# Attention weights spread by transfers from SBUF to SBUF instead of matmuls and copies, in three chunks of four

## The chip, the cores and the metric

One Trainium2 chip, one core. The time is device time in microseconds (us) of one execution, as a median over runs. PE is the matrix engine (TensorE), PEld its weight loads, DVE the vector engine, ACT the scalar engine, POOL the GpSimd engine, SP the engine that only issues transfers. Each engine works through its own queue strictly in order and waits on semaphores for the others. Matmuls write to PSUM, of which there are eight banks of 128 x 512 float32.

## The reference

A transformer layer on 2048 positions of width 512, in bfloat16: attention over a sliding window, then a gated MLP, each after a layer norm and with a residual.

```python
qkv = (x @ wqkv)...                         # 32 heads of 16
off = jnp.arange(8) * 2                     # W = 8 places back, step 2
logits = einsum("bhsd,bhswd->bhsw", q, kg) * scale     # kg: k at pos - off
attn = softmax(where(mask, logits, -1e9))
o = einsum("bhsw,bhswd->bhsd", attn, vg)    # then @ wo
...
h = x + A(layernorm(x));  gate = relu(layernorm(h) @ W_gate)
h2 = h + (gate * (layernorm(h) @ W_up)) @ W_down       # F = 1376
```

Each position sees only itself and seven earlier positions, two apart. So scores and weighted sums are element-wise products of shifted rows, not matmuls of queries by keys.

## The kernel before

The 2048 positions are cut into four chunks of 512 (`tk` 0 to 3). Within a chunk, activations stand transposed: features on partitions, positions along the row. The features are put in an order such that one tile (t = 0 to 3) of 128 partitions holds 4 of each head's 16 dimensions, partition 4h + q belonging to head h.

Per chunk the steps are, with their names in the code (`key`, written here as step and chunk, mu3.2 for `mu`, tile 3, chunk 2):

- Layer norm of x: `xst`, `xag` (DVE statistics), `xrl`, `xre` (ACT, reciprocal root as exp of a log), `xxn` (DVE, normalised rows), then the transpose: `xtp` on PE with `xte` on ACT, or `xtd` as a transposing DMA issued by SP (L472). The list DMAT names which pairs of blocks go by DMA: x of chunk 3, h of chunks 2 and 3, and half of h of chunk 1 (`htd`).
- Projections `qkv0` to `qkv11` (L524; q and k first, then v) with their copies `qe` on ACT (L532).
- Scores: `pr0`, `pr1` (two each, DVE, L571) multiply q by four shifted views of k, 128 x 4096 at a time, into a `big` buffer; `sc0`, `sc1` (PE, L577) sum over dimensions with 0/1 weights, in column tiles of 32; `ex0`, `ex1` take the exponential, giving two tiles `ex`, in which partition 32w + h holds the weight of window place w and head h.
- Normalisation: `den` (PE, L610) sums over the places, `dl` and `dr` (ACT) make the reciprocal; in chunks 1 to 3 (EARLY) `am0`, `am1` (DVE, L625) multiply the weights by it.
- Spread: the weights of a place stand on 32 partitions, one per head, and are wanted on 128, each four times. `bc0`, `bc1` (PE, L638) do it with four matmuls each, on row tiles of 32, into four PSUM banks; `be` (ACT, L644, four for each) copies the banks into a `big` buffer `ab` of 128 x 8 x 512.
- Weighted sum: `mu0` to `mu3` (DVE, L659) multiply `ab` by eight shifted views of v into a `big` buffer each; a tree of adds follows (`tree`, 4 + 2 + 1 wide; L662, L685). In chunks 0 to 2 (DACC) the first, widest add is an accumulating DMA issued by POOL (`ta`, L691, 512 KB).
- `wo` (PE, L711) and the residual `rs`, layer norm of h (`hnm`, `hsq`, `hrl`, `hre`, `hxn`, `htp` or `htd`), then the MLP: `mm` (PE, L749, up and gate, 22 steps of four matmuls), `ue`, `ge` (ACT), `gu` (DVE), `dn` (PE, L786, two parts for each of four row blocks), `o` (DVE, L797, adds the residual) and `os` (a store, L801).

The order is not that of the loops. Every step is added to a plan with its engine, duration, latency, buffers taken and used; the list RANK gives each step a place, in the order in which steps are added. Each engine's queue is its steps sorted by RANK. `Plan.order` then walks the queues with the planned durations, only to choose which buffer of a pool a step gets and in which order the program is written. So planned costs do not change an engine's order as long as RANK is there. Pools that matter here: five `big` buffers (products of scores, `ab`, and products with v share them), eight PSUM banks.

The last chunk's last row block is stored in two halves (`parts`), so the stores there are `os0` to `os4`.

Of the kernel before, what the change touches and what calls it, by code (L numbers as in the profile page):

```python
# [8 lines left out]
P = 128  # L9
BF16 = mybir.dt.bfloat16  # L10
# [3 lines left out]
ALU = mybir.AluOpType  # L14
# [4 lines left out]
    0, 1, 2, 3, 4, 5, 6, 7, 8, 9, 10, 11, 12, 13, 14, 15, 16, 18, 19, 24,  # L19
    26, 31, 32, 17, 20, 22, 23, 25, 29, 34, 35, 28, 33, 37, 39, 41, 45, 48, 21, 27,  # L20
    30, 36, 38, 42, 44, 46, 63, 74, 40, 56, 68, 49, 51, 54, 43, 60, 72, 53, 66, 65,
    77, 70, 83, 75, 80, 90, 92, 87, 114, 102, 110, 85, 105, 93, 104, 115, 125, 129, 78, 88,
    95, 99, 103, 183, 193, 202, 132, 143, 150, 156, 152, 106, 109, 116, 123, 119, 168, 181, 216, 220,
    224, 180, 188, 217, 223, 231, 187, 196, 226, 229, 234, 162, 172, 201, 205, 207, 237, 240, 239, 245,
    247, 251, 242, 248, 243, 246, 252, 256, 259, 263, 250, 254, 265, 266, 272, 278, 269, 276, 285, 275,
    283, 273, 280, 286, 318, 322, 292, 301, 304, 314, 313, 324, 341, 311, 325, 298, 303, 334, 338, 326,
    330, 346, 354, 360, 337, 355, 317, 353, 347, 358, 370, 329, 352, 340, 348, 332, 345, 294, 350, 356,
    361, 374, 343, 365, 372, 381, 351, 362, 413, 357, 368, 367, 386, 418, 400, 425, 460, 464, 417, 427,
    457, 467, 376, 434, 446, 466, 410, 429, 437, 668, 55, 61, 52, 57, 50, 58, 47, 59, 62, 64,
    67, 84, 73, 82, 86, 71, 81, 69, 79, 89, 166, 175, 122, 136, 111, 130, 137, 190, 91, 101,  # L30
    127, 173, 149, 179, 94, 96, 163, 213, 158, 170, 98, 107, 108, 167, 208, 197, 249, 257, 244, 235,
    255, 260, 264, 268, 274, 296, 279, 302, 309, 305, 310, 307, 287, 295, 290, 293, 300, 319, 328, 364,
    369, 315, 320, 359, 363, 335, 342, 380, 382, 327, 336, 373, 375, 389, 395, 387, 392, 396, 402, 393,
    399, 398, 401, 397, 403, 405, 409, 404, 407, 411, 412, 416, 419, 420, 423, 421, 428, 422, 426, 431,
    474, 482, 441, 443, 458, 463, 453, 468, 483, 438, 448, 436, 452, 442, 451, 450, 454, 456, 488, 492,
    479, 498, 455, 487, 491, 500, 507, 461, 493, 445, 459, 481, 485, 471, 475, 496, 511, 539, 524, 533,
    520, 535, 526, 530, 541, 514, 540, 484, 502, 543, 544, 556, 581, 589, 538, 552, 559, 562, 549, 554,
    584, 587, 529, 547, 560, 564, 113, 120, 100, 124, 76, 117, 97, 112, 128, 133, 140, 144, 142, 146,
    164, 145, 154, 148, 157, 161, 209, 230, 174, 186, 198, 200, 195, 215, 182, 184, 199, 228, 189, 211,
    169, 177, 178, 194, 232, 241, 271, 281, 185, 191, 261, 253, 284, 297, 289, 282, 308, 312, 321, 331,  # L40
    339, 344, 378, 366, 377, 371, 379, 383, 385, 394, 388, 391, 390, 430, 439, 470, 490, 424, 432, 473,
    476, 440, 447, 486, 489, 406, 415, 465, 477, 501, 518, 497, 504, 508, 512, 494, 499, 521, 525, 517,
    519, 516, 522, 503, 505, 527, 528, 532, 546, 534, 537, 536, 548, 531, 542, 579, 597, 566, 594, 585,
    601, 561, 580, 609, 599, 603, 588, 592, 571, 575, 577, 600, 605, 606, 610, 595, 623, 602, 611, 582,
    614, 627, 558, 576, 574, 578, 568, 572, 565, 567, 583, 621, 648, 639, 645, 636, 649, 591, 616, 652,
    624, 635, 628, 633, 640, 655, 663, 665, 667, 632, 654, 661, 711, 650, 656, 707, 710, 644, 657, 659,
    669, 126, 138, 118, 134, 131, 139, 121, 135, 141, 147, 155, 160, 151, 171, 159, 165, 153, 176, 203,
    236, 218, 225, 192, 204, 214, 219, 258, 291, 262, 270, 222, 233, 267, 277, 227, 238, 212, 221, 288,
    316, 206, 210, 306, 299, 323, 333, 384, 349, 408, 414, 433, 435, 444, 462, 449, 506, 510, 509, 513,
    515, 469, 495, 478, 472, 480, 563, 570, 586, 593, 523, 551, 557, 569, 573, 590, 596, 598, 545, 550,  # L50
    553, 555, 615, 622, 604, 607, 612, 619, 608, 613, 626, 629, 618, 620, 630, 631, 617, 625, 634, 637,
    638, 641, 646, 653, 643, 651, 642, 647, 691, 695, 681, 692, 694, 698, 688, 697, 700, 679, 687, 674,
    677, 670, 680, 666, 671, 690, 673, 675, 672, 682, 658, 662, 660, 678, 683, 684, 689, 664, 685, 699,
    702, 676, 693, 705, 701, 706, 704, 709, 686, 703, 708, 713, 715, 716, 718, 696, 714, 719, 720, 722,
    724, 731, 712, 726, 732, 734, 717, 725, 727, 730, 728, 733, 735, 737, 721, 723, 729, 736,
# [3 lines left out]
class Op:  # L59


    __slots__ = ("eng", "dur", "lat", "fn", "deps", "prio", "take", "use", "start", "done", "seq", "key")

    def __init__(self, eng, dur, fn, deps=(), prio=0.0, take=(), use=(), lat=0.0):
        self.eng, self.dur, self.fn, self.lat = eng, dur, fn, lat
        self.deps = [d for d in deps if d is not None]
        self.prio, self.take, self.use = prio, list(take), list(use)
        self.start = self.done = None
# [23 lines left out]
class Plan:  # L92
# [23 lines left out]
    def order(self):  # L116
# [14 lines left out]
        while left:  # L131
# [36 lines left out]
            op.start, op.done = t, t + op.dur + op.lat  # L168
            free[op.eng] = t + op.dur
# [18 lines left out]
def kernel(  # L188
# [20 lines left out]
    PADL = 16  # L209
    SCALE = DH ** -0.5  # L210
# [45 lines left out]
    big_s = slots(5, [P, W, CS], BF16, "big")  # L256
    gT_s = slots(7, [P, 2, CS], BF16, "gT")
    ex_s = slots(3, [P, CS], BF16, "ex")
    ln_s = slots(1, [P, CS], F32, "lnd")
# [81 lines left out]

    RPE, OPE = (0,), ()
# [5 lines left out]
    HG = ([[0, 1, 2, 3]],) * 4  # L348

# [3 lines left out]
    MM, TP = 0.2165, 0.07  # L353
    SW = 0.22
    PEL = 0.22
    A5, A10, AX, AS = 0.52, 0.92, 0.8, 0.24
    AL = 0.14
    D2, D5, D10, D20, D40, DST, DSM = 0.34, 0.62, 0.62, 1.15, 2.2, 0.63, 0.08
    DXN = 0.38
    DL = 0.14  # L360

    def load(t):
        return add(None, "LD", 0.0, None, lat=t)

    xload = [[load(t) for t in (3.4, 3.4, 4.2, 4.2)]] + [[load(t)] * BPC for t in (9.5, 14.0, 15.5)]
    wload = {n: load(t) for n, t in
             (("q", 8.0), ("k", 8.0), ("v", 12.0), ("o", 17.5), ("u", 21.5), ("g", 25.5), ("d", 29.5))}
# [17 lines left out]
    def layernorm(tk, src, dst_slots, pr, groups, on_act, residual=None):  # L385
# [7 lines left out]
        for grp in groups:  # L393
# [3 lines left out]
            for j in grp:  # L397
                if residual:
# [14 lines left out]
                    ag.append(add((ln + "sq" + gk, tk), "ACT", A5 + 0.1 if h else 0.73, f_sq, [a], pr,  # L413
# [52 lines left out]
            for j0 in range(lo, hi, step):  # L466
                if (ln, tk, j0) in DMAT:
                    for j in range(j0, min(j0 + step, hi)):
                        xn, a = norm(j)

                        def f_td(j=j, xn=xn):
                            nc.sync.dma_start_transpose(out=dst.t[:, :, j * P:(j + 1) * P], in_=xn.t[:])  # L472

                        evs.append(add((ln + "td" + gk, tk), "SP", TDD, f_td, [a], pr, take=[dst], use=[xn], lat=TDL))
                    continue
# [25 lines left out]
                evs.append(add((ln + ("tv" if tev else "te") + gk, tk), "DVE" if tev else "ACT", A10 if n == 2 else A5, f_ev, ds, pr, take=[dst], use=[tp], lat=AL))  # L501
# [5 lines left out]
    for tk in range(NCK):  # L507
# [49 lines left out]
        for hf in range(2):  # L557
# [26 lines left out]
            if tk in MERGE:  # L584
# [23 lines left out]
        def f_dn(exs=exs, dn=dn, tk=tk):  # L608
            for hf in range(2):
                nc.tensor.matmul(dn.t[:], lhsT=(same if tk in EARLY else spread)[:], rhs=exs[hf].t[:], start=(hf == 0), stop=(hf == 1))  # L610
# [7 lines left out]
        b = add(("den", tk), "PE", 2 * MM, f_dn, exd, apr + 2, take=[dn], use=exs, lat=PEL)  # L618
# [11 lines left out]
        ab, abd = Buf(big_s), []  # L630
        for w0 in range(0, W, BCN):
            hf = w0 // 4
            bcs = [Buf(at_s) for _ in range(BCN)]
# [17 lines left out]
        for t in range(NT):  # L651
# [35 lines left out]
            for n, du in ((4, D20), (2, D10), (1, D2)):  # L687
                f = lambda n=n, mt=mt, f=f_a: f(n, mt)
                if n == 4 and (tk, t) in DACC:
# [3 lines left out]
                    m = add(("ta%d" % t, tk), "POOL", 1.5, f_da, [m], tpr, use=[mt], lat=DAL)  # L693
# [3 lines left out]
                else:  # L697
                    m = add(("tree%d" % t, tk), "DVE", du, f, [m], tpr, use=[mt], lat=0.03)
# [7 lines left out]
        for j in range(BPC):  # L706
# [20 lines left out]
            if tk in RPE:  # L727
                a = add(("rs%d" % j, tk), "ACT", A5 + 0.1, f_rs, [a], base + 50, take=[sm], use=[od], lat=AL)
            else:
                a = add(("rs%d" % j, tk), "DVE", D5 + 0.1, f_rs, [a], base + 50, take=[sm], use=[od], lat=DL)  # L730
# [7 lines left out]
        for f0 in range(0, NFT, 2):  # L738
# [3 lines left out]
            for ft in fts:  # L742
# [4 lines left out]
                def f_mm(w_sb, mm, ft=ft, fs=fs, hnT=hnT):  # L747
                    for dt in range(NT):
                        nc.tensor.matmul(mm.t[:fs, :], lhsT=w_sb[:, dt, ft * P: ft * P + fs],  # L749
                                         rhs=hnT.t[:, dt, :], start=(dt == 0), stop=(dt == NT - 1))  # L750
# [4 lines left out]
                def f_ge(gm=gm, gr=gr, fs=fs, i=ft - f0):  # L755
                    nc.scalar.activation(out=gr.t[:fs, i, :], in_=gm.t[:fs, :], func=ACT.Relu)  # L756

                a = add(("mm%d" % (f0 // 2), tk), "PE", 4 * MM, lambda f=f_mm, um=um: f(wu_sb, um), hev + [wload["u"]], pr,
                        take=[um], use=[hnT], lat=PEL)
# [94 lines left out]
```

## Time and profile before

| | |
|---|---|
| time, median of 3 runs | 203.77 us (203.76 to 203.87) |
| span of the profiled execution | 200.7 us, 3.1 us less than the median time |
| granted PE clock | 0.999 |
| last matmul ends | 197.17 us |
| L638 spread matmuls | x32 (8 steps of 4) |
| L644 copies of the spread banks, ACT | x32, 17.8 us busy |
| L691 accumulating transfers, POOL | x12, 512 KB, 5.6 us from issue to landing |
| L801 stores, SP | x17, issue 0.33 to 0.48 us, 1.6 to 1.9 us to landing |
| L472 transposes, SP | x14, issue 1.20 to 2.14 us, 2.4 to 5.6 us to landing |

The page gives the span, from the first to the last instruction of the profiled execution, but no separate time for it; the difference of 3.1 us to the median of the runs lies around the span. In the lines below, a group is: line, engine, operation, output tile <- input tiles, shape, count; in the timeline the first two numbers are the start and the time in us, and the bracket tells how long the engine had idled and for whom. In the slices each digit is the busy tenth of one fortieth of the span, about 5 us. In the waits: engine, line, whom it waited for, total us, times, longest.

### The profile page before, as it was taken

How to read it: one execution, taken by the hardware profiler on the slowest of the kernel's cores; microseconds unless marked ns; L12 is line 12 of the kernel's file. 1: busy time of each engine (PE TensorE's matmuls, PEld its weight loads, DVE VectorE, ACT ScalarE, POOL GpSimd, SP SyncE). 2: the span in 40 equal slices, each digit the busy share in tenths (PEclk: the TensorE clock that was granted, in tenths of full speed). 3: DMA queues.
4: the chain of work that ended last, by engine and by line, in shares of the span. 5: the costliest groups of instructions: out<-in, count | busy, mean ns of one | idle time of the engine just before them, and what ended most of it. 6: DMA issues, size and time to landing. Idle time of an engine off the chain costs nothing.

```text
span 200.7 us, 2938 instructions
## 1 busy us (share of the span) xinstructions
PE 193.4 (96%) x1095; PEld 96.2 (48%) x1115; DVE 153.3 (76%) x239; ACT 121.8 (61%) x256; POOL 12.7 (6%) x28
## 2 busy tenths in 40 slices
PE   8999999989999999999999999999999999999992
PEld 8776445445445344444444444444444444444451
DVE  6989998989999999999996868799967412022313
ACT  3576798747899965887436779701566631277400
POOL 4000000410000013100131000000000000000000
PEclk9999999999999999999999999999999999999999
DMA  6989933994000009920399400131010050200103
GB/s 204 322 245 409 388 119 66 170 201 87 3 0 0 3 0 183 195 40 3 57 178 193 124 3 0 29 75 52 3 52 0 0 104 3 78 0 0 52 0 105
DMA packets 17676, 18.81 MB, mean 94 GB/s; under 512 B 8352, under 2 KB 14464, under 8 KB 17664
## 3 DMA queue, kind: packets, MB, share of 16 engines
q1 hardware_dynamic: 15360, 11.57, 18.5%
q0 software_dynamic: 1728, 6.29, 16.6%
q10 hardware_dynamic: 576, 0.79, 1.2%
q8 instruction: 8, 0.13, 0.3%
q14 instruction: 4, 0.03, 0.0%
HBM read 8.42 MB, written 2.10 MB: 52 GB/s over the span
## 4 chain that ended last, share of the span: by engine, by line
PE 67%; DVE 16%; DMA 6%; ACT 5%; issue 2%; SPq 1%; ACTq 0%
PE bank L749 29%; PE bank L524 15%; PE bank L786 14%; DVE big L659 6%; PE bank L711 5%; DMA quad<-row 5%; DVE big L571 3%; DVE gT L769 2%; DMA x_sm<-in_A_x_dram 1%; SPq L472 1%; PE bank L483 1%; DVE x_sm L722 1%; DVE big L662 1%; DVE row L454 1%; PE bank L577 1%
## 5 line engine op out<-in xcount | busy, mean ns | idle before, releaser
L749 PE MATMUL bank<-quad,wu_sb 128*128 128x512 bf16 (+1 forms) x172 | 42.4, 379 | 0.4
L749 PE MATMUL bank<-quad,wg_sb 128*128 128x512 bf16 (+1 forms) x173 | 42.0, 379 | 0.4 <-DMA quad<-row 0.3
L756 ACT ACTIVATE gr<-bank 128x512 bf16<-128x512 f32 (+1 forms) x44 | 25.3, 616 | 24.7 <-PE bank L749 22.9
L786 PE MATMUL bank<-wd_sb,gT 128*128 128x512 bf16 (+2 forms) x183 | 39.8, 366 | 0.2
L753 ACT CAST up_sb<-bank 128x512 bf16<-128x512 f32 (+1 forms) x44 | 25.0, 600 | 21.0 <-PE bank L749 17.3
L571 DVE TENSOR_TENSOR big<-quad,kT 128x4096 bf16<-128x4096 bf16 x16 | 36.2, 2284 | 0.2
L659 DVE TENSOR_TENSOR big<-big,vT 128x4096 bf16<-128x4096 bf16 x16 | 35.9, 2281 | 0.0
L769 DVE TENSOR_TENSOR gT<-gr,up_sb 128x1024 bf16<-128x1024 bf16 (+1 forms) x24 | 15.3, 642 | 24.0 <-ACT up_sb L753 14.4
L524 PE MATMUL bank<-quad,wqk_sb 128*128 128x512 bf16 (+1 forms) x139 | 29.9, 355 | 1.0 <-DMA quad<-row 0.8
L786 PEld LDWEIGHTS <-gT 128*128 128x128 bf16 (+1 forms) x187 | 18.1, 98 | 19.7 <-issue 0.4
L749 PEld LDWEIGHTS <-wg_sb 128*128 128x128 bf16 (+1 forms) x176 | 17.3, 100 | 21.2 <-issue 0.9
L749 PEld LDWEIGHTS <-wu_sb 128*128 128x128 bf16 (+1 forms) x176 | 17.5, 100 | 20.6 <-issue 0.7
L524 PEld LDWEIGHTS <-wqk_sb 128*128 128x128 bf16 x144 | 15.6, 114 | 12.8 <-issue 2.3
L797 DVE TENSOR_TENSOR row<-x_sm,bank 128x512 bf16<-128x512 bf16 (+1 forms) x17 | 10.6, 649 | 10.4 <-PE bank L786 10.4
L644 ACT CAST big<-bank 128x512 bf16<-128x512 f32 x32 | 17.8, 635 | 0.4 <-PE bank L638 0.2
L662 DVE TENSOR_TENSOR big<-big 128x1024 bf16<-128x1024 bf16 (+2 forms) x24 | 16.8, 728 | 0.1
L691 POOL DMA_DIRECT2D big<-big x12 | 10.5, 873 | 88.1 <-DVE big L659 59.9
L524 PE MATMUL bank<-quad,wv_sb 128*128 128x512 bf16 x62 | 15.6, 380 | 0.2
L711 PE MATMUL bank<-wo_sb,quad 128*128 128x512 bf16 x62 | 15.2, 379 | 0.2
L454 DVE TENSOR_SCALAR row<-x_sm,mv,rs 128x512 bf16<-128x512 bf16 x32 | 11.4, 407 | 3.7 <-ACT rs L436 3.1
L532 ACT CAST quad<-bank 128x512 bf16<-128x512 f32 x16 | 9.5, 612 | 4.6 <-PE bank L524 4.6
L499 ACT COPY quad<-bank 128x1024 bf16<-128x1024 bf16 (+1 forms) x9 | 8.0, 929 | 6.0 <-PE bank L483 6.0
(68 smaller groups left out, 147.2 us busy)
## 6 DMA issues: line engine op xcount, KB each, us to landing
big<-big POOLq DMA_DIRECT2D x12, 512.0 KB, 5.6
out_dram<-row SPq DMA_DIRECT2D x15, 128.0 KB, 1.8
x_sm<-in_A_x_dram SPq DMA_DIRECT2D x3, 512.0 KB, 5.5
wu_sb<-in_B_W_up_dram SPq DMA_DIRECT2D x1, 1376.0 KB, 8.6
wg_sb<-in_B_W_gate_dram SPq DMA_DIRECT2D x1, 1376.0 KB, 11.6
wd_sb<-in_B_W_down_dram SPq DMA_DIRECT2D x1, 1280.0 KB, 14.9
wqk_sb<-in_A_wqkv_dram ACTq DMA_DIRECT2D x2, 256.0 KB, 5.0
wqk_sb<-in_A_wqkv_dram SPq DMA_DIRECT2D x2, 256.0 KB, 5.2
```

Source lines behind the costliest of these rows:

```text
L454: V.tensor_scalar(out=xn.t[:], in0=x, scalar1=mv.t[:, j, 0:1], scalar2=rs.t[:, j:j + 1], op0=ALU.add if residual else ALU.subtract, op1=AL ...
L524: nc.tensor.matmul(mm.t[:, lo:hi], lhsT=wv_sb[:, dt, t:D:NT] if c == 2 else wqk_sb[:, dt, c * D + t:(c + 1) * D:NT], rhs=xnT.t[:, dt, lo:h ...
L571: V.tensor_tensor(out=pb.t[:].rearrange("p (t w) s -> p t w s", t=2), in0=q4, in1=k4, op=ALU.mult)
L644: nc.scalar.copy(out=ab.t[:, w, :], in_=bc.t[:])
L659: V.tensor_tensor(out=mt.t[:], in0=ab.t[:], in1=v8, op=ALU.mult)
L662: V.tensor_tensor(out=mt.t[:, 0:n, :], in0=mt.t[:, 0:n, :], in1=mt.t[:, n:2 * n, :], op=ALU.add)
L711: nc.tensor.matmul(od.t[:], lhsT=OT.t[:, t, j * P:(j + 1) * P], rhs=wo_sb[:, t, :], start=(t == 0), stop=(t == NT - 1 and tk not in RPE))
L749: nc.tensor.matmul(mm.t[:fs, :], lhsT=w_sb[:, dt, ft * P: ft * P + fs], rhs=hnT.t[:, dt, :], start=(dt == 0), stop=(dt == NT - 1))
L753: nc.scalar.copy(out=ub.t[:fs, i, :], in_=um.t[:fs, :])
L756: nc.scalar.activation(out=gr.t[:fs, i, :], in_=gm.t[:fs, :], func=ACT.Relu)
L769: V.tensor_tensor(out=gt.t[:fs, 0:n, :], in0=gr.t[:fs, 0:n, :], in1=ub.t[:fs, 0:n, :], op=ALU.mult)
L786: nc.tensor.matmul(od.t[:, c0:c1], lhsT=gts[ft].t[:fs, ft % 2, j * P:(j + 1) * P], rhs=wd_sb[:fs, ft, c0:c1], start=(ft == 0), stop=(ft == ...
```

## The change

For chunks 1 to 3 the steps `bc` and `be` are gone. In their place is one step `bd` for each half (`bd0`, `bd1`): SP issues four transfers, each from the 32 partitions of one place of `ex`, read four times over, to the 128 partitions of one slice of `ab`, 128 KB in rows of 1 KB. Chunk 0 keeps the matmuls and copies. The very last store is issued by ACT instead of SP. The planned durations are set anew, the plan gets one shared DMA queue (`dq`), and RANK is a new list of 714 places (738 before: 30 steps gone, 6 added). Other options come in as code but are off: DEN1, PRE and HSP are empty and NAB is 0.

```diff
+    BCD = {(1,0):"SSSS",(1,1):"SSSS",(2,0):"SSSS",(2,1):"SSSS",(3,0):"SSSS",(3,1):"SSSS"}
+    BDI = {"S": 0.63, "A": 0.65, "P": 0.95}
...
+            if op.dq:
+                at = max(t + op.dur + op.dq[0], free.get("DQ", 0.0)) + op.dq[1]
+                free["DQ"] = at
+                op.done = at + op.lat
...
-    MM, TP = 0.2165, 0.07
-    SW = 0.22
+    MM, TP = 0.2165, 0.057
+    SW = 0.21
...
-        ab, abd = Buf(big_s), []
+        ab, abd = Buf(ab_s), []
         for w0 in range(0, W, BCN):
             hf = w0 // 4
+            if (tk, hf) in BCD:
+                for eng, q in (("SP", nc.sync), ("ACT", nc.scalar), ("POOL", nc.gpsimd)):
+                    ws = [w for w in range(4) if BCD[tk, hf][w] == eng[0]]
+                    if not ws:
+                        continue
+
+                    def f_bd(ws=ws, q=q, w0=w0, ab=ab, ex=exs[hf]):
+                        for w in ws:
+                            q.dma_start(ab.t[:, w0 + w, :], ex.t[w * HB:(w + 1) * HB, :].unsqueeze(1).to_broadcast([HB, 4, CS]))
+
+                    abd.append(add(("bd%d%s" % (hf, eng[0]), tk), eng, len(ws) * BDI[eng[0]], f_bd, [exd[hf]], apr + 1,
+                                   take=[ab], use=[exs[hf]], lat=0.77, dq=(0.75 - 0.5 * (len(ws) - 1), 0.5 * len(ws))))
+                continue
             bcs = [Buf(at_s) for _ in range(BCN)]
...
+            last = tk == NCK - 1 and n == len(parts) - 1
+
-            def f_os(j=j, c0=c0, c1=c1, ob=ob, tk=tk):
-                nc.sync.dma_start(out_rows[:, tk * BPC + j, c0:c1], ob.t[:, c0:c1])
+            def f_os(j=j, c0=c0, c1=c1, ob=ob, tk=tk, q=nc.scalar if last else nc.sync):
+                q.dma_start(out_rows[:, tk * BPC + j, c0:c1], ob.t[:, c0:c1])
```

With NAB 0, `ab_s` is the pool `big_s` as before. The queues that the two RANK lists give, where they bear on what follows (x4: four times in a row):

```
SP before    xtd.3 x4, htd.1 x2, os0.0 os2.0 os1.0, htd.2 x4, os1.1 os3.1 os2.1 os0.1, htd.3 x4, os0.2 os3.0 os3.2 os2.2 os1.2 os2.3 os0.3 os1.3 os4.3 os3.3
SP after     xtd.3 x4, bd0.1 bd1.1 bd1.2 bd0.2, htd.1 x2, bd1.3, os1.0, bd0.3, os0.0 os3.0, htd.2 x4, os3.1 os0.1 os2.0 os1.1, htd.3, os2.1, htd.3 x3, os0.2 os2.2 os3.2 os1.3 os3.3 os0.3 os1.2 os2.3
ACT after    ... ge4.3 ue4.3 ue4.3 ge5.3 ue5.3 ge4.3 os4.3
DVE before   ... mu3.0 mu0.0 mu1.0 mu2.0 pr0.1 ... hxn.0 x4, am1.1 pr1.2 pr1.2 am0.1 pr0.3 pr0.3 mu1.1 mu0.1 mu3.1 mu2.1 gu0.0 am0.2 gu1.0 pr1.3 gu3.0 (tree 1, 0) gu2.0 (tree 3) am1.2 (tree 2) pr1.3 rs1.1 rs0.1 hnm hnm rs3.1 rs2.1 hnm hnm mu3.2 gu4.0 hxn.1 gu5.0 hxn.1 x3, mu1.2 mu0.2
DVE after    ... xxn.3 x3, mu3.0 xxn.3 mu2.0 ... hnm.0 pr0.2 am0.1 hxn.0 x4, am1.1 pr0.2 pr0.3 pr0.3 mu1.1 mu0.1 mu3.1 mu2.1 gu0.0 am1.2 pr1.3 gu2.0 tree0.1 am0.2 (trees, gu3.0, gu1.0; tree 2 last) pr1.3 rs2.1 rs0.1 rs1.1 hnm hnm mu3.2 hnm rs3.1 hnm gu4.0 gu5.0 hxn.1 x4, mu0.2 ... am1.3 (trees) gu2.1 am0.3 o1.0 (trees) ... mu1.3
PE before    ... den.0 qkv11.2 qkv6.2 qkv2.3 ... wo2.0 sc0.1 sc1.1 ... sc0.2 bc1.1 ... dn2.0 bc1.2 wo1.1 wo0.1 wo3.1 wo2.1 dn0.0 sc1.3 dn3.0 dn1.0 dn0.0 htp.1 dn1.0 htp.1 dn3.0 den.3 dn2.0 mm1.1
PE after     ... qkv6.2 den.0 qkv0.3 ... sc0.1 wo1.0 wo3.0 wo2.0 wo0.0 sc1.1 ... dn2.0 wo2.1 wo0.1 wo1.1 sc1.3 wo3.1 dn3.0 dn1.0 den.3 dn3.0 dn0.0 htp.1 htp.1 dn1.0 dn0.0 dn2.0 mm2.1
```

## The prediction

> Steps are named as in the code: mu3.2 is step `mu`, tile 3, chunk 2; where a name occurs several times I say which. The order of each engine's queue is read from the two RANK lists, matched to the steps in the order in which they are added.
>
> **What bounds the kernel now.** First the page's busy shares and the slices:
>
> ```profile
> PE 193.4 (96%) x1095; PEld 96.2 (48%) x1115; DVE 153.3 (76%) x239; ACT 121.8 (61%) x256; POOL 12.7 (6%) x28
> PE   8999999989999999999999999999999999999992
> DVE  6989998989999999999996868799967412022313
> PEclk9999999999999999999999999999999999999999
> ```
>
> PE is full from the second slice to the next to last, at full clock; DVE is as full only until about 110 us. "Busy" could hide waiting, so the second view is PE's own waits:
>
> ```profile
> PE bank L373 <- DVE warm L287: 1.0, 1, 1.0
> PE bank L524 <- DMA quad<-row: 0.8, 1, 0.8
> PE bank L483 <- DVE row L454: 0.5, 1, 0.5
> PE bank L749 <- DMA quad<-row: 0.3, 1, 0.3
> ```
>
> After the start only two waits are left, both for a transpose by DMA. So the time is PE's queue: its work, plus these waits, plus the tail of 3.5 us after the last matmul (197.17 of 200.7). An edit counts if it takes PE work out, or moves a wait. That the chain of waits runs through DVE from 69 to 100 us only says that the wait at 103.67 goes back to DVE.
>
> Third, the timeline of PE around one spread:
>
> ```profile
> 83.72 2.11 PE L749 MATMUL bank<-quad,wu_sb 128*128 128x512 bf16 x9
> 85.76 0.39 PE L638 MATMUL bank<-ex,spread 32*128 32x512 bf16 x4
> 86.09 1.06 PE L749 MATMUL bank<-quad,wg_sb 128*96 128x512 bf16 x4
> ```
>
> Nine matmuls from 83.72, 0.2165 us apart, put the last start at 85.45; the next ordinary one starts at 86.09. That is 0.64 us where 0.2165 would pass without the spread: one spread costs 0.42 us of PE.
>
> Fourth, two places where PE waits, and the tail on DVE:
>
> ```profile
> 38.80 1.03 PE L524 MATMUL bank<-quad,wqk_sb 128*128 128x512 bf16 x4
> 40.64 1.68 PE L524 MATMUL bank<-quad,wqk_sb 128*128 128x512 bf16 x7 [0.82 <-DMA quad<-row]
> ...
> 102.56 0.81 PE L786 MATMUL bank<-wd_sb,gT 128*128 128x512 bf16 x3
> 103.67 1.02 PE L749 MATMUL bank<-quad,wg_sb 128*128 128x512 bf16 x4 [0.30 <-DMA quad<-row]
> ...
> 197.20 0.42 DVE L797 TENSOR_TENSOR row<-x_sm,bank 128x256 bf16<-128x256 bf16 x1 [0.24 <-PE bank L786]
> ```
>
> Start to start, less one matmul, the first costs 0.98 us (39.45 to 40.64) and the second 0.46.
>
> **The change, part by part.** All against the span of 200.7 us; the times before lie 3.1 us above it (203.77), and I keep that offset.
>
> *PE.* Six spreads go: five at 0.42, and bc1.1, which follows scores (narrow tiles already) and costs 0.32: 2.42. The scores sc0.1 and sc1.1, adjacent before, are now apart. The pair took 55.97 to 58.12 less one matmul, 1.93; sc1.0 alone took 1.07; two alone 2.14: +0.21. Net -2.21.
>
> *ACT.* 24 copies go, 0.49 us apart: 11.8 us, from 64 to 125 us. ACT is 61% busy and no wait of PE names it: no gain by itself. What it opens is that ACT frees PSUM banks earlier.
>
> *SP.* 24 transfers of 128 KB come in. Their issue: the stores of the same size take 0.33 to 0.48 us each on SP, the transposes 1.2 to 2.1. I take 0.45, the diff's planner 0.63. Landing 1.8 us after issue (stores), so a half of four lands 3.2 to 3.7 us after its `am`. Engine time: the store packets of 1 KB took 44 ns, 128 of them over 16 engines 0.35 us; the far end is 2.8 us, a 512 KB accumulating transfer. Stores write HBM, these read 32 partitions four times over, so I take 0.5. SP's new queue is xtd.3 x4, bd0.1, bd1.1, bd1.2, bd0.2, htd.1 x2, bd1.3, os1.0, bd0.3, os0.0, os3.0, htd.2 x4. Behind each wait:
> - bd0.1, bd1.1 wait for the two `am`; from am1.1 to mu1.1 DVE has pr0.2, pr0.3, pr0.3, 6.6 us. The 3.7 us are covered; no accumulating transfer is in flight then. Cost 0.
> - bd1.2 also needs a `big` buffer: four products, one `pr1.3` and this one are six for five. It waits for the second tree step of tile 0, about 4 us after am1.2. Then two halves, 8 issues, 3.6 to 5.0 us, and 1.8 us to land: about 8.4 after am1.2 by the low issue price, 11 by the high. mu3.2 comes 12.5 us after am1.2 on DVE. Cost 0, cover 1.5 to 4.
> - htd.1 waits behind these, but its rows are normalised 3 us after mu3.2 starts. Cost 0.
> - bd0.3 waits behind os1.0, whose o1.0 follows am0.3 by 0.6 us on DVE; mu1.3 comes some 8 us later. htd.2 stands behind os0.0 and os3.0, both long ready. Cost 0.
>
> *The wait at 40.6.* The new PE queue has seven projection steps of chunk 2 ahead of the first of chunk 3, where six stood: 0.87 us more. mu3.0 is now ahead of the last xxn.3, so the accumulating ta3.0 starts earlier, but the transpose that comes last is paced by SP's issue (34.86). 0.98 falls to 0.1: -0.88.
>
> *The hand-over to wo.1.* wo1.1 began at 90.00 and its last input (the tree's last add of tile 2) ended at 90.04: no slack before. PE now gets there earlier by its removed work (1.3 net up to there) and the wait (0.88): 87.8. DVE does the same steps up to there; its idle that the new order fills is 0.57 (last xxn.3, waiting for a row buffer), 0.47 (om3.0, for the reciprocal) and 0.44 (hnm.0), and pr1.0 placed ahead of xxn.1 costs about 0.4 anew: 1.1 earlier, 88.95. New PE wait: +1.15. Bounds: 0 if DVE's own waits shrink further, 3.9 if the accumulating transfers land later by the eight spread transfers' engine time (8 x 0.35 = 2.8).
>
> *The wait at 103.67.* From the end of the last wo.1 PE has 8.7 us of other work (down projections 7.8, two transposes 0.45, den.3 0.43) to the first mm.1. wo.1 in three steps, sc1.3 and wo3.1 end at 93.5, so mm.1 is due at 102.15. The path to it: rs3.1 must wait for mu3.2 (to 95.3), hnm, ACT's square and two small ones (1.5), hxn.1 at 97.5, second transpose issued 99.3, landing 2.5 later, 101.8. It fits with 0.3: the 0.46 goes: -0.46. Both sides: 0 gained, or a wait of 1.7 (transposes held behind an accumulating transfer as before, 103.5 at 3.4 us after issue).
>
> The chunks after that have more cover: the filler between the last wo.2 and mm.2 is 13.4 us (13.6 before, when the transposes landed 2.1 early), between wo.3 and mm.3 13.0 (13.2, 1.9 early). Cost 0, with 1 us as the far end.
>
> *Small hand-overs in chunk 0.* sc1.0, bc1.0, sc0.0 and bc0.0 are due 0.87 us earlier on PE, with 0.1 to 0.4 us left over DVE's steps by my count: +0.2 (0 to 0.9).
>
> *The tail.* The last store was issued at 197.96 though its add ended at 197.62: SP was still issuing the store before (197.41 + 0.45). From ACT's queue, idle since 190: -0.34. ACT's issue took 0.38 to 0.46 where it was used at the start, as SP's. The last part is still a half tile.
>
> Sum: -2.21 - 0.88 + 1.15 - 0.46 + 0.2 - 0.34 = -2.54. Span 198.2, time 201.3 us (203.77 - 2.54 = 201.23, rounded up).
>
> *A rule against the change.* Between 99.2 and 101.6 us the DMA view shows only the accumulating queue at work, although transposes had been issued from SP at 98.31; they ran once it was done. Between 36.3 and 38.5 it shows both, SP's queue at 22%. The Trainium skill, "DMA: Bandwidth & Descriptors", section "Queues, rings and completion order", says that each DMA engine takes turns between queues, packet by packet. By that rule the spreads of chunk 2 would slow the accumulating transfers of chunk 1 and the wait at wo.1 would be 3.9 instead of 1.15: some 204.0 us. By the first row the spreads wait, and nothing is lost. The two rows are split; the buffer wait above keeps bd1.2 out of most of that stretch, so I go by the first.
>
> **The rivals.**
> 1. *No new wait at wo.1.* DVE keeps up. For: it loses three idle spots; against: zero slack before. 201.3 - 1.15 = 200.1.
> 2. *Part of the gain is lost.* wo.1 or mm.1 wait 1 to 2 us more (accumulating transfers slowed, or mu3.2 late by a spread): 202.2 to 203.3. For: the thin 0.3 and 1.5 us covers.
> 3. *Slower: the spread transfers are slow.* Engine time per transfer far above the store's, since each reads 32 partitions four times. A half takes four; mu1.1 has 6.6 us of cover, and bd0.1 goes ahead by only about 3 us, so both halves must fit in about 9.6: eight transfers over 1.0 us each begin to cost DVE time. At 2.8 us each (the accumulating row) eight take 22.4, mu1.1 comes some 14 us late, of which PE's filler hides a part; with half of it showing, 208. The gains of 3.9 us (2.21 + 0.88 + 0.46 + 0.34) are used up at about 1.5 us per transfer. Against: the store row of 0.35.
> 4. *No change that can be told* (within 0.2%, about 0.4 us, what a measurement of this kernel can tell): new waits of 3.5 to 4.3 us: the far end of the wait at wo.1, 3.9.
>
> **How the numbers follow.** The forecast (200.6 to 202.2) 0.50; rival 1 (below 200.6) 0.13; rival 2 (to 203.36) 0.16; rival 4 0.07; rival 3 and others above 0.14. Faster 0.79, same 0.07, slower 0.14. The range runs from 199.7 (rival 1 with some of the small terms at 0) to 203.5 (rival 2 whole, the edge of rival 4): it leaves out about 0.03 below and 0.16 above. The forecast's own range is 200.6 to 202.2.
>
> **What the profile after would show.** The L638 group x8 instead of x32, the L644 casts x8; PE busy near 191; the wait for quad<-row at the first chunk-3 projection gone or under 0.3; a new PE wait at wo.1 of about 1 us; transfers of 128 KB big<-ex on SP landing in about 2 us; the last store on ACT. I am wrong if these land much later than 2 us, if DVE shows a wait before L659 of over 1 us, or if PE's waits after the start sum to over 3 us.

## The result, and the profile after

| | before | changed |
|---|---|---|
| time, median of 20 runs each | 203.72 us (203.26 to 204.09) | 201.91 us (201.35 to 204.15) |
| ratio, 95% interval | | 0.9908 [0.9888, 0.9928] |

The changed kernel is 1.8 us faster; 2.5 were forecast (201.3), within a range of 199.7 to 203.5. Ratios leave out executions in a slower state of the chip; below, one of e8 is such (203.28 us, clock 0.989; the median of its other five is 200.56 us). The trace that came with the result is that of its slowest run (204.15 us, span 202.4). The unchanged file was therefore traced once more, run e1_again below (201.06 us, span 199.3), and the lines here are from that trace unless said otherwise. First the busy shares and the slices of its page; line numbers have moved, L689 and L695 are the old L638 and L644, L762 is `wo`, L800 `mm`, L845 `dn`, L710 `mu`:

```profile
PE 193.1 (97%) x1091; PEld 95.4 (48%) x1091; DVE 152.4 (76%) x239; ACT 111.2 (56%) x232; POOL 12.7 (6%) x28
PE   8899999999999999999999999999999999999994
DVE  6789999998999989999899769999965511141332
PEclk9999999999999999999999999999999999999999
```

The change did what it says. Of the spreads and their copies only chunk 0's are left, and the transfers are there (groups and list of transfers, same trace):

```profile
L695 ACT CAST big<-bank 128x512 bf16<-128x512 f32 x8 | 4.5, 595 | 0.1
L689 PE MATMUL bank<-ex,spread 32*128 32x512 bf16 x8 | 0.8, 384 | 0.0
...
big<-ex SPq DMA_DIRECT2D x24, 128.0 KB, 3.4
```

Then PE's waits, to be held against the four of before:

```profile
PE bank L385 <- DVE warm L296: 1.0, 1, 1.0
PE bank L536 <- DVE quad L509: 0.4, 1, 0.4
PE bank L536 <- ACT rs L444: 0.4, 1, 0.4
PE bank L800 <- ACT quad L511: 0.4, 1, 0.4
PE bank L762 <- DVE quad L717: 0.3, 1, 0.3
PE bank L762 <- DVE quad L736: 0.2, 1, 0.2
PE bank L589 <- DVE mv L412: 0.2, 1, 0.2
```

Both waits for a transpose (`quad<-row`, at the chunk-3 projections and at mm.1) are gone. In their place stand small ones, nearly all for something that DVE or ACT makes in chunk 0 or 1: at wo.0 (L717), at the first mm.0 (L511), at the score (L589) and at wo.1 (L736).

To see where the time went, each trace is cut at three points on PE: the start of the first wo.0, the start of the first mm.1, and the end of the last matmul. All are read from matmul rows; us.

| trace | time of that run | start to wo.0 | wo.0 to mm.1 | mm.1 to last matmul | tail |
|---|---|---|---|---|---|
| before, first | | 51.87 | 51.81 | 93.48 | 3.52 |
| before, second (e5) | 203.36 | 52.72 | 51.87 | 93.49 | 3.52 |
| changed, first | 204.15 | 54.24 | 52.58 | 92.62 | 2.94 |
| changed, second (e1) | 201.06 | 51.45 | 52.28 | 92.62 | 2.94 |

The last two columns repeat to 0.01 us: 0.87 less after mm.1, which is two spreads, and 0.58 less in the tail. Together 1.45 of the 1.81 us. The first two columns are to be added for this comparison, as wo.0 has another place in the new queue: up to mm.1 the change is worth only some 0.4 us by the medians (1.81 - 1.45), where the prediction had 1.36. Four of the six spreads and both removed waits lie there.

### The profile page after: what moved, and what is told of

Same layout as the page of the kernel before. It is cut to its first block, busy times and chain, and to the rows that moved or that the text cites. A ratio compares the mean times of both kernels' runs of the same rounds, so it can differ in the third digit from the quotient of the medians.

```text
span 202.4 us, 2934 instructions
## 1 busy us (share of the span) xinstructions
PE 194.1 (96%) x1072; PEld 97.0 (48%) x1091; DVE 152.8 (75%) x239; ACT 111.1 (55%) x232; POOL 12.7 (6%) x28
## 4 chain that ended last, share of the span: by engine, by line
PE 67%; DVE 12%; DMA 10%; issue 4%; ACT 4%; POOL 1%; SPq 1%; DVEq 0%; POOLq 0%; ACTq 0%
PE bank L800 29%; PE bank L845 18%; PE bank L536 11%; PE bank L762 5%; DVE big L710 5%; DVE big L583 4%; DMA big<-big 4%; DMA wqk_sb<-in_A_wqkv_dram 4%; PE bank L589 2%; DMA big<-ex 2%; ACT kT L544 2%; PE bank L495 1%; DVE row L466 1%; ACT quad L511 1%; POOL big L742 1%
## 5 line engine op out<-in xcount | busy, mean ns | idle before, releaser
L800 PE MATMUL bank<-quad,wu_sb 128*128 128x512 bf16 (+1 forms) x173 | 43.0, 379 | 0.7 <-ACT quad L511 0.4
L800 PE MATMUL bank<-quad,wg_sb 128*128 128x512 bf16 (+1 forms) x172 | 42.4, 379 | 0.1
L845 PE MATMUL bank<-wd_sb,gT 128*128 128x512 bf16 (+2 forms) x182 | 39.9, 366 | 0.4
L710 DVE TENSOR_TENSOR big<-big,vT 128x4096 bf16<-128x4096 bf16 x16 | 36.1, 2285 | 0.8 <-DMA big<-ex 0.8
L536 PE MATMUL bank<-quad,wqk_sb 128*128 128x512 bf16 (+1 forms) x140 | 31.4, 368 | 2.1 <-DMA wqk_sb<-in_A_wqkv_dram 1.9
L845 PEld LDWEIGHTS <-gT 128*128 128x128 bf16 (+1 forms) x187 | 18.2, 98 | 20.1 <-DVE gT L828 0.6
L800 PEld LDWEIGHTS <-wu_sb 128*128 128x128 bf16 (+1 forms) x176 | 17.6, 100 | 21.0 <-DMA big<-ex 0.4
L800 PEld LDWEIGHTS <-wg_sb 128*128 128x128 bf16 (+1 forms) x176 | 17.4, 100 | 21.0 <-issue 1.3
L536 PEld LDWEIGHTS <-wqk_sb 128*128 128x128 bf16 x144 | 16.1, 117 | 14.5 <-DMA wqk_sb<-in_A_wqkv_dram 2.2
L762 PE MATMUL bank<-wo_sb,quad 128*128 128x512 bf16 x63 | 15.4, 380 | 0.8 <-DVE quad L736 0.4
L431 DVE BATCH_NORM_STATS2 st<-x_sm 128x6 f32<-128x512 bf16 x16 | 10.6, 672 | 3.2 <-DMA x_sm<-in_A_x_dram 3.2
L511 ACT COPY quad<-bank 128x1024 bf16<-128x1024 bf16 (+1 forms) x9 | 8.1, 921 | 8.5 <-PE bank L495 8.5
L544 ACT CAST kT<-bank 128x512 bf16<-128x512 f32 x16 | 9.1, 598 | 4.8 <-DVE big L583 3.5
```

Of the source, the lines that this page charges most:

```text
L536: nc.tensor.matmul(mm.t[:, lo:hi], lhsT=wv_sb[:, dt, t:D:NT] if c == 2 else wqk_sb[:, dt, c * D + t:(c + 1) * D:NT], rhs=xnT.t[:, dt, lo:h ...
L544: nc.scalar.copy(out=o, in_=mm.t[:])
L710: V.tensor_tensor(out=mt.t[:], in0=ab.t[:], in1=v8, op=ALU.mult)
L762: nc.tensor.matmul(od.t[:], lhsT=OT.t[:, t, j * P:(j + 1) * P], rhs=wo_sb[:, t, :], start=(t == 0), stop=(t == NT - 1 and tk not in RPE))
L800: nc.tensor.matmul(mm.t[:fs, lo:hi], lhsT=w_sb[:, dt, ft * P: ft * P + fs], rhs=hnT.t[:, dt, lo:hi], start=(dt == 0), stop=(dt == NT - 1))
L845: nc.tensor.matmul(od.t[:, c0:c1], lhsT=gts[ft].t[:fs, ft % 2, j * P:(j + 1) * P], rhs=wd_sb[:fs, ft, c0:c1], start=(ft == 0), stop=(ft == ...
```

## The experiments

Each run's ratio is to the kernel before, run beside it on the same chip. In queue diffs only the moved steps and their neighbours are shown.

### The changed kernel, the old order, and the work put back

**e1_again** is the changed file with no edit.

> The changed kernel once more, unedited, to have a trace in which the first weights arrive as early as in the profile of before (in the first trace of the changed kernel PE waited 1.9 us for them, and its span of 202.4 is 2.3 above that of its other runs). All theories: about 201.9 us, span near 200.1, last matmul about 3.0 us before the end of the span (3.5 before the change).

201.66 us (6 runs), 0.9910 [0.9886, 0.9935]: the result again, and the trace used above.

**e2_old_order** has the transfers, but each queue in the order of before. The steps `bc` and `be` drop out, `bd` come in where SP can issue them, am0.2 stands two places later, and all stores are on SP.

```diff
-SP  xtd.3 x4, htd.1 x2, os0.0 os2.0 os1.0, htd.2 x4, ...
+SP  xtd.3 x4, bd1.1 bd0.1 bd0.2 bd1.2, htd.1 x2, bd1.3, os0.0 os2.0 os1.0, bd0.3, htd.2 x4, ...
-PE  ... bc0.1 ... bc1.1 ... bc0.2 ... bc1.2 ...   ACT ... be0.1 x4 ...
+last = False
```

> The transfers alone: every engine keeps the order it had before, the spreads and copies of chunks 1 to 3 are taken out, the transfers are put into SP's queue where their inputs came ready, all stores stay on SP; the one other move is the multiply am0.2, two places later. Theory 'PE work': the first four spreads (1.6 us of PE) are given back as waiting at wo.1, where PE had no slack over DVE, the two of chunk 3 (0.84) stay gained: 202.5 to 203.1 us, and a PE wait of 1 to 2 us appears before wo.1. Rival 'the order': taking the spreads out is worth nothing by itself: 203.4 to 204.0.

204.07 us (12 runs), 1.0023 [1.0000, 1.0047]: no gain, if anything 0.5 us slower. Its PE waits:

```profile
PE bank L800 <- ACT up_sb L804: 1.8, 1, 1.8
PE bank L800 <- DMA quad<-row: 1.1, 1, 1.1
PE bank L536 <- DMA wqk_sb<-in_A_wqkv_dram: 1.0, 1, 1.0
...
PE bank L762 <- DVE quad L736: 0.8, 1, 0.8
PE bank L536 <- DMA quad<-row: 0.7, 1, 0.7
```

PE has lost the same work as in the changed kernel (mm.1 to the last matmul is 92.62 here too), but it stands 1.8 us inside mm.0, 0.8 at wo.1 and 1.1 at mm.1. DVE had waited 1.4 us at mu1.1, because in the old order the second of chunk 1's two `am` comes so late that its four transfers, issued from 68.45 to 71.22, land only at 73.82; the chain of what ended last runs through DVE from 74 to 92 us in this trace. The theory that removed PE work is worth its full price wherever it is removed has fallen.

**e3_work_back** is the changed kernel with the PE work of the spreads put back, without the spread: two plain matmuls (0.43 us) at each of six places, whose result nobody reads.

```diff
+                bx = Buf(at_s)
+
+                def f_bx(bx=bx, ex=exs[hf]):
+                    for n in range(2):
+                        nc.tensor.matmul(bx.t[:], lhsT=spread[:], rhs=ex.t[:], start=True, stop=True)
```

> The changed kernel with 0.43 us of PE work (two matmuls whose result nobody reads) put back at each of the six places where a spread would stand, nothing else changed. Theory 'PE work': 2.6 us more work, of which up to 1.0 falls into the waits that PE now has before wo.1: 203.5 to 204.5 us. Rival 'DVE or the transfers are the bound now': PE has room, at most +0.5: below 202.4.

203.03 us (12 runs), 0.9975 [0.9956, 0.9993]. Of 2.60 us put back 1.37 show in the time. The stages say which: wo.0 to mm.1 is 52.70 against 52.28, that is 0.42 for four places with 1.73 us of work; mm.1 to the last matmul is 93.48 against 92.62, 0.86 for two places with 0.87. So in this kernel three quarters of PE's saving before mm.1, if not more (the first trace of the changed kernel has 52.58 there), are given back as waits; after mm.1 all of it counts.

### What sets the pace before mm.1

**e9_dve_work** (on the kernel of e4_swap below, 200.81 us) gives DVE four more operations of 128x512, two ahead of am1.1 and two ahead of am1.2. They take the maximum of the weights with themselves and change no value.

```diff
+                if hf == 1 and tk in (1, 2):
+                    def f_bv(ex=exs[hf]):
+                        for n in range(2):
+                            V.tensor_tensor(out=ex.t[:], in0=ex.t[:], in1=ex.t[:], op=ALU.max)
```

> Base: the exchange of the two bd steps of chunk 2 (200.8 us). DVE gets four more operations of 128x512 that change no value (the weights' maximum with themselves): two ahead of am1.1, two ahead of am1.2, both before the first mm.1; pitch of such an operation in the trace 0.34 us, so 1.36 us of work. 'DVE sets the pace up to the first mm.1': all of it returns, the stage from the first wo.0 to the first mm.1 goes from 51.2 to 52.4-52.7 and the time to 201.9-202.3. Rival 'PE sets the pace there too, DVE has slack': PE has 0.3 us of waits in that stage, most of the 1.36 lies in it, the time stays at 200.7-201.2.

202.00 us (12 runs), 0.9939 [0.9915, 0.9964], 1.2 us above e4_swap. The timeline of DVE and, after it, of PE in this run:

```profile
64.35 0.88 DVE L668 TENSOR_TENSOR ex<-ex 128x512 bf16<-128x512 bf16 x2
65.26 0.43 DVE L663 TENSOR_TENSOR ex<-ex,rec 128x512 bf16<-128x512 bf16 x1
...
82.01 0.88 DVE L668 TENSOR_TENSOR ex<-ex 128x512 bf16<-128x512 bf16 x2
82.99 0.42 DVE L663 TENSOR_TENSOR ex<-ex,rec 128x512 bf16<-128x512 bf16 x1
```

```profile
67.94 1.05 PE L589 MATMUL bank<-big,sel 128*32 128x512 bf16 x16 [0.66 <-DVE big L583]
...
89.95 1.47 PE L851 MATMUL bank<-wd_sb,gT 128*128 128x512 bf16 x6 [0.73 <-DVE gT L834]
```

The four cost more than I had taken, 0.91 + 0.98 = 1.89 us (the starts of the next operation less their own), and wo.0 to mm.1 grows from 51.40 to 53.14, by 1.74. PE meets the delay in two waits for DVE. By the medians, which carry the spread of the start as well, 1.2 of the 1.89 show. So in the kernel of e4_swap DVE has next to no slack up to mm.1.

This is not a price to be set beside PE's 0.42 of 1.73 (e3). That run stands on the changed kernel, where PE waits more in this stage: by the starts of matmuls 1.6 us after wo.0 in e1_again, 0.9 in e4_swap. PE work added to e4_swap was not run. The chain of what ended last lies on PE alone from 60 us on in e3, on DVE until 89.9 in e9, and on PE again from 67 us on in e4_swap (lines below). So two paths of nearly the same length lead to mm.1, PE's queue on one side, DVE's steps and the transfers between them on the other, and a saving on one shows only until the other is the longer.

**e10_fill_wo0** (on e4_swap) moves a PE step into PE's wait at wo.0.

```diff
-PE  sc0.1 wo1.0 wo3.0 wo2.0 wo0.0 sc1.1 qkv2.3 qkv11.3
+PE  sc0.1 qkv2.3 wo1.0 wo3.0 wo2.0 wo0.0 sc1.1 qkv11.3
```

> Base as in the run before. PE's step qkv2.3 (four matmuls, 0.87 us) is moved ahead of wo1.0, where PE waits 0.50 us for DVE's om0.0 and then 0.31 at sc1.1. 'DVE sets the pace': nothing gained, since wo2.1 waits for DVE's tree anyway: 200.6-201.0. Rival 'these waits of PE count': both go, 0.5 to 0.8 less: 200.0-200.3.

201.24 us (4 runs), 0.9892 [0.9868, 0.9916]: nothing gained, 0.2 above the upper end of what DVE's pace had led me to write. The waits at wo.0 and at the score are gone, and PE has a new one instead, the first of these lines (the second is in e4_swap as well):

```profile
PE bank L495 <- DVE row L466: 0.5, 1, 0.5
PE bank L800 <- ACT quad L511: 0.4, 1, 0.4
```

The new one is before the transposition of chunk 0's normalised rows. The first mm.1 starts at 103.62 us, where e4_swap has 103.82.

**e8_chunk0_too** (on e4_swap) makes chunk 0's spreads transfers as well.

```diff
-    BCD = {(1,0):"SSSS",...
+    BCD = {(0,0):"SSSS",(0,1):"SSSS",(1,0):"SSSS",...
-SP  xtd.3 x4, ...
+SP  bd1.0 bd0.0, xtd.3 x4, ...
```

> The swapped kernel with chunk 0 spread by transfers as well: two more spreads (0.84 us of PE) and eight copies (3.9 us of ACT) go. Theory 'DVE sets the pace up to the first mm.1': nothing gained, 200.6 to 201.1, since DVE's steps are the same. Rival 'PE work': 200.0. Second rival: these transfers queue behind the weight loads, which run until 28 us, and mu3.0 comes later: 201.2 or more.

200.69 us (6 runs), 0.9865 [0.9823, 0.9907], against 200.88 for e6_last_store_sp in the same series: no gain that can be told. DVE waits 1.7 us for the transfers where chunk 0 has no other work for it, and PE gives its saving back at wo.0 (waits of DVE, then of PE):

```profile
DVE big L710 <- DMA big<-ex: 1.7, 1, 1.7
```

```profile
PE bank L762 <- DVE quad L717: 1.8, 1, 1.8
PE bank L800 <- ACT quad L511: 0.4, 1, 0.4
```

### Transfers that meet

**e4_swap** exchanges two steps in SP's queue. bd1.2 could be issued at once when am1.2 was done, beside the accumulating transfers of chunk 1; bd0.2 must wait until the tree of tile 0 has freed its part of the buffer, and holds bd1.2 back if it goes first.

```diff
-SP  bd0.1 bd1.1 bd1.2 bd0.2 htd.1 x2
+SP  bd0.1 bd1.1 bd0.2 bd1.2 htd.1 x2
```

> In SP's queue of the changed kernel, bd0.2 (whose buffer is free only when the tree of tile 0 is done) before bd1.2, so that no spread transfer runs beside the last accumulating transfer of chunk 1. Theory 'shared DMA engines': that transfer lands some 2 us earlier, DVE's wait before the tree of tile 2 (0.8 us) and most of PE's wait at wo.1 go: 201.0 to 201.5 us. Rival 'the accumulating transfers are late by themselves': landing unchanged, 201.9. Second rival: the spreads now come too late for mu3.2, and DVE waits there instead: 202.2 or more.

200.81 us (5 runs), 0.9870 [0.9846, 0.9893], 0.85 less than e1_again in the same series; wo.0 to mm.1 goes from 52.28 to 51.40. It beats both kernels. The timelines of POOL, SP and DVE show the mechanism. The changed kernel, e1_again:

```profile
81.42 0.86 POOL L742 DMA_DIRECT2D big<-big  x1 [1.34 <-DVE big L710]
82.31 8.52 SPq L679 DMA_DIRECT2D big<-ex  x8
89.37 0.69 DVE L713 TENSOR_TENSOR big<-big 128x1024 bf16<-128x1024 bf16 x1 [0.49 <-DMA big<-big]
```

With the exchange, e4_swap:

```profile
81.73 0.86 POOL L742 DMA_DIRECT2D big<-big  x1 [1.34 <-DVE big L710]
86.60 5.09 SPq L679 DMA_DIRECT2D big<-ex  x8
89.11 0.69 DVE L713 TENSOR_TENSOR big<-big 128x1024 bf16<-128x1024 bf16 x1
```

The last accumulating transfer of chunk 1 is issued at about the same time in both. Beside the spread transfers it lands at 89.35, 7.9 us after its issue (8.2 in the first trace), nearly alone at 87.95, 6.2 us (6.2 before the change, too). DVE's add waits for it, and wo.1 for that add. The eight issues on SP, 5.09 us here, take 8.52 beside the accumulating transfers: single ones rise from 0.55 to 1.5 and 2.0 us. And the spreads gain nothing by going early: issued at 82.31, the first lands at 89.55; issued at 86.60, at 89.17.

The chain of what ended last before mm.1 shows what the exchange changes. In e1_again it goes from PE to chunk 1's spreads, through DVE to the late accumulating transfer and back to PE at wo.1; in e4_swap it stays on PE:

```profile
67.91 3.90 DMA big<-ex
...
81.42 7.93 DMA big<-big
89.37 0.69 DVE big L713
90.06 0.35 DVE quad L736
90.46 2.67 PE bank L762 x11
```

```profile
69.31 2.70 PE bank L800 x12
...
76.00 13.06 PE bank L800 x60
89.06 1.73 PE bank L845 x8
90.78 2.59 PE bank L762 x12
```

Not all of the 0.88 between these two traces need be the exchange: DVE also waits 0.8 us at mu1.1 in e1_again and about 0.1 in e4_swap, ahead of the exchanged steps. The trace of e12_xst1_only, which has the exchange and waits 0.7 us at mu1.1, has 51.67 from wo.0 to mm.1, still 0.61 less.

The list of transfer queues from 88 to 90 us in the first trace of the changed kernel shows how the two share the engines (q0 holds the accumulating transfers, q1 what SP issues; packets, MB, share of 16 engines):

```profile
q0 software_dynamic: 77, 0.32, 87.5%
q1 hardware_dynamic: 76, 0.08, 15.2%
```

77 packets of one and 76 of the other, as many of each, as turns would give (77 and 74 between 85 and 87 us in e1_again). But a packet of q0 has 4 KB and one of q1 has 1 KB, so the spread transfers get a fifth of the bytes, and still take 15% of the engines' time from the other. The Trainium skill, "DMA: Bandwidth & Descriptors", section "Queues, rings and completion order", says that an engine takes turns between queues packet by packet. The equal counts agree; the order on a single engine, and whether a packet there is one of those counted here, no row shows.

**e7_am_early** (on e4_swap) tries the other remedy for late transfers, at chunk 1: `dl.1`, `dr.1` on ACT and am0.1, am1.1 on DVE some 2 us earlier, so that mu1.1 need not wait for the spreads (0.8 us in e1_again).

```diff
-DVE pr0.2 am0.1 hxn.0 x4 am1.1 pr0.2 pr0.3 pr0.3 mu1.1
+DVE am0.1 am1.1 pr0.2 hxn.0 x4 pr0.2 pr0.3 pr0.3 mu1.1
```

> The swapped kernel with the reciprocal of chunk 1 (dl.1, dr.1 on ACT) and its two multiplies (am0.1, am1.1 on DVE) about 2 us earlier, so that the spreads of chunk 1 land before mu1.1 needs them in every run (they landed 0.8 us after that in two traces, in time in the swapped one). Theory 'DVE sets the pace up to the first mm.1': 200.2 to 200.8, no DVE wait before mu1.1. Rival 'PE sets it there': 200.8, nothing gained. Second rival: hsq on ACT comes later and holds up hxn.0: 201.0 or more.

201.69 us (8 runs), 0.9916 [0.9887, 0.9944], 0.8 more than e6_last_store_sp beside it. The second rival had it: the rows of chunk 0 are normalised later, PE waits for them, and the delay stays to the end (wo.0 to mm.1 is 51.99, against 51.41 in e6). Its timeline of PE at that place:

```profile
65.07 1.37 PE L495 MATMUL bank<-identity,row 128*128 128x128 bf16 x16 [0.45 <-DVE row L466]
```

### The tail, the start, and the kernel before

**e6_last_store_sp** (on e4_swap) puts the last store back on SP.

```diff
-            last = tk == NCK - 1 and n == len(parts) - 1
+            last = False
```

> The swapped kernel (bd0.2 before bd1.2) with the last store on SP again. My forecast gave ACT's queue 0.34 us: then 201.1 against 200.8. Rival: with the new order SP has issued the store before at least 0.4 us before the last add ends, so SP is free then and the queue is worth nothing: 200.8, the last store issued within 0.1 us of the last add.

200.88 us (6 runs), 0.9877 [0.9836, 0.9919], as e4_swap; tail 2.92 us. The ACT queue is worth nothing. The rows say why. In e1_again the last add and the last store from ACT, and ahead of them the last stores from SP:

```profile
193.51 2.71 SPq L862 DMA_DIRECT2D out_dram<-row  x5
196.38 0.42 DVE L856 TENSOR_TENSOR row<-x_sm,bank 128x256 bf16<-128x256 bf16 x1 [0.52 <-PE bank L845]
196.84 0.35 ACTq L862 DMA_DIRECT2D out_dram<-row  x1
```

SP is free at 196.22 (193.51 + 2.71), 0.6 us before it would be needed. Before, SP issued os1.3, os4.3 and os3.3 back to back at the very end, after the add of a full tile (o1.3) that came just ahead of the last half. In the new order the last half tile's add comes later than all other stores are issued, from whichever queue. So 0.30 of the tail's 0.58 us comes with the new order of the last steps, not with the queue: the last store is issued 0.80 us after the last matmul before, 0.50 in e1_again, 0.49 in e6. Nearly all of the other part lies between the landing of that store and the end of the span, 1.13 us before and 0.89 in e1_again; e2, with the old order and SP, has 0.91, so it is not the order's or the queue's, and its cause stays open.

**e5_before_again** is the kernel before, traced once more.

> The kernel before, unedited, for a second trace: in the first one the weights came without a wait of PE, in all five traces taken since PE waits 0.9 to 1.9 us for them at 8 to 10 us. If that wait is a matter of the single execution, it is here too in part, and the span is 201.3 to 202.3; if the changed kernels bring it, it is not here and the span is 200.7 again.

203.36 us, span 201.6. Its waits inside the chunks are close to those of the first trace (by the starts of matmuls 0.53 us at mm.1 and 0.89 at the chunk-3 projections, 0.46 and 0.98 there), its start is 0.85 us longer, and PE waits 0.8 us for its weights: that wait is a matter of the single execution.

**e11_start_order** and **e12_xst1_only** (on e4_swap) try the start. In the new order DVE stands at xst.1 for the load of x of chunk 1, with a copy of chunk 0 behind it. e12 makes the first edit alone, e11 both.

```diff
-DVE xxn2.0 xst.1 xtv3.0 xst.1 xag.1
+DVE xxn2.0 xtv3.0 xst.1 xst.1 xag.1
-DVE xag.1 xst.2 pr1.0 xxn.1
+DVE xag.1 pr1.0 xst.2 xxn.1
```

> Base: the exchange of the two bd steps of chunk 2 (200.8 us). In DVE's queue the first xst.1 goes behind the copy xtv3.0 and the first xst.2 behind the first pr1.0. In the traces of the new order DVE stands 1.1 to 2.9 us at xst.1 for the load of x of chunk 1, with the copy of chunk 0's transpose behind it (PE then waits 0.2 to 0.5 for that copy), and another 0.6 to 0.8 at xst.2 for the next load, with pr1.0 behind it. The order of before had both later and waited 0.4 to 0.6 at the start. 'DVE's pace from the start on': pr1.0 starts 0.6 to 1.0 earlier and all after it: 199.8 to 200.2. Rival 'the start is hidden by later work': 200.6 to 201.0.

> As the run before, but only xst.1 goes behind the copy. pr1.0 still stands behind xst.2 and its wait for the load, so 'DVE's pace' expects 0 to 0.2 us: 200.6 to 200.9. Rival 'the copy is what PE and the rest wait for': nearly the whole gain, 199.9 to 200.3.

200.49 us (6 runs), 0.9876 [0.9836, 0.9916], and 200.76 us (6 runs), 0.9859 [0.9830, 0.9888]: neither can be told from e4_swap, and the gain that I wrote for e11 is not there. In e11's trace (DVE, then PE) the copy itself now waits, for PE, and PE waits for its weights:

```profile
10.29 0.43 DVE L509 COPY quad<-bank 128x512 bf16<-128x512 bf16 x1 [2.08 <-PE bank L495]
```

```profile
8.86 0.94 PE L536 MATMUL bank<-quad,wqk_sb 128*128 128x256 bf16 x6 [0.78 <-DMA wqk_sb<-in_A_wqkv_dram]
```

Two loads arrive at about the same time, and with DVE's steps moved back the other is still waited for (in e4_swap both are, 1.1 us on PE as well). Over the traces with the changed kernel's order of the start, wo.0 begins between 51.37 and 54.24 us, later where DVE's wait for x was longer (1.1 us in e9, 2.9 in the first trace). The first trace has a second reason: its granted clock was 0.50 from 10 to 12 us and 0.67 from 12 to 14, where the others have 1.00. Without it the latest start is 52.85 us (e8). That is why single traces of one kernel differ by more than the changes do, and why the stages after wo.0 are compared here.

## Why the prediction was right or wrong

The direction, the removed waits and the price of a spread were right; the size was 0.7 us too large, because the spread transfers land late and slow the accumulating ones, both of which the sum had at nothing. By its own steps:

- **PE, -2.21.** The two spreads of chunk 3 return 0.87 us (0.84 by my 0.42). The four before mm.1, with the two removed waits, are 2.71 us of the sum and could not show whole: DVE's path to wo.1 had no slack, as the sum says, with its new wait there. In the changed kernel that path became longer by the meeting transfers, and three quarters of the PE work put back there are hidden (e3).
- **The wait at 40.6, -0.88, and the wait at 103.67, -0.46.** Both are gone, as said. Since they lie before mm.1, what they saved went the way of those four spreads.
- **The hand-over to wo.1, +1.15.** In e1_again PE waits 0.58 us there and just before (by the starts of matmuls: 0.25 at the down projection, 0.33 at wo.1). The step that failed is the decision on the accumulating transfers: I took the row in which transposes ran only once the accumulating queue was done, and left the rule of taking turns aside. The rows above are the rule's. The price was less than the rule's case had it (3.9 us in place of 1.15): 1.7 to 2.0 us later landing, 0.85 us of time (e4). The reason given for keeping bd1.2 out of that stretch was wrong as well. By the times, its buffer is waited for slice by slice: in the first trace bd1.2 is issued at 85.14, just after the accumulating transfer of tile 0 landed at 85.00, almost 4 us before that tile's second tree step ends on DVE at 88.98.
- **SP's transfers, cost 0 for mu1.1.** The issue pitch is 0.65 us, not 0.45, the landing 2.7 us after issue when alone, not 1.8, and the last two of eight come 3.9 to 4.2 us after theirs in e1_again. mu1.1 waited 0.8 us. The rival of slow transfers (1.0 us each and more) is out: the first six of eight land 0.6 to 0.8 us apart. One of the signs set for being wrong came, a landing much later than 2 us (median 3.4); the other two did not, with 0.8 us of DVE before L710 and 1.1 us of PE's waits after the start.
- **Small hand-overs in chunk 0, +0.2.** Three waits between wo.0 and mm.0 instead, of 0.3, 0.2 and 0.4 us by the waits view (L717, L589, L511): 0.9, the upper end of what was allowed.
- **The tail, -0.34.** It was -0.58: 0.30 by the earlier last store, and nearly all of the rest behind its landing, which the sum did not have and which is luck. I read the 0.34 rightly as SP being busy, but did not ask whether the new order of the last steps removes that by itself; it does, and the queue is worth nothing (e6).
- **The offset of 3.1 us.** It was hardly a property of the kernel. In most runs whose own time is known, the span is 1.8 us below it (203.36 and 201.6, 201.06 and 199.3; up to 3.2 in single ones). The first trace of before, 200.7, most likely belonged to a short execution, of some 202.5 us. The sum of differences did not suffer from this.
- **PE busy near 191 us.** The page has 193.1. The page of before lacks 20 records of matmuls (1095, with 1115 weight loads), so its 193.4 is too low to be held against it.

In sums: after mm.1 and in the tail 1.18 were forecast and 1.45 came; up to mm.1 1.36 were forecast and some 0.4 came, and the exchange of e4, which keeps the two kinds of transfers apart, brings 0.85 more. That is most of what was missing before mm.1, and more than the whole shortfall of 0.7.

What stays open: the new order with the spreads still on PE was not run, nor was PE work put back into the kernel of e4_swap. So the order's own part is known only from both sides: transfers in the old order gain nothing (e2), and the new order with PE's work put back is at 0.9975 (e3).

## What to carry to other kernels

A busy share of 96% names the bound of the whole, not of each stage: before work is taken off PE, ask in which stage another engine's path is nearly as long, and count the saving there only up to the difference; adding a known cost to one engine and then to the other measures the slack of each, if both are added to the same kernel (e3 and e9 were not). A transfer that is issued early into a stretch where a large transfer is in flight can land no sooner and delay the large one (here by 1.7 us); the order in a single queue can be used to hold it back, here without a new wait on DVE. And when a queue is changed for one instruction, look first at whether the new order has left the old queue free.

## What was not expected of the hardware

- Issuing is not a fixed cost: the same 128 KB transfer takes SP 0.55 us to issue alone, and, after a first one of 0.54, 1.1 to 2.0 us while accumulating transfers of 512 KB are in flight (e1_again, 82.95 to 87.8 us).
- Small packets suffer much from sharing the engines, large ones less: 77 against 76 packets in 2 us, 0.32 against 0.08 MB; the small transfers land 4.7 to 7.5 us after issue instead of 2.7, the large one 7.9 to 8.2 instead of 6.2.
- Of eight such transfers in a row, with no other data transfer beside them, the last two can land 3.2 to 4.3 us after issue, the others after 2.5 to 2.8 (chunk 1's spreads in both traces of the changed kernel and in e4_swap). The eight of chunk 2 in e4_swap all land after 2.5 to 2.7; what delays the two is open.
- The start of wo.0 moves by up to 2.8 us from one execution to the next of the same file (51.45 and 54.24), with the arrival of the first loads and, in the later one, a granted clock of 0.50 and 0.67 between 10 and 14 us; the two parts were not separated.
